# A recurrent-attention and spatial-gating kernel whose instructions are issued from a table: the table is replaced

## The chip, the cores and the metric

The kernel runs on one core of one Trainium2 chip. The core has five engines with a queue each: PE (TensorE, matmuls), DVE (VectorE), ACT (ScalarE), POOL (GpSimd) and SP (SyncE, which here issues every DMA). Each engine takes its instructions strictly in the order in which they were issued to it. PEld is PE's loading of the stationary operand. The metric is device time in microseconds (us), lower is better.

## What is computed

Batch 4, 8 heads, 768 steps, head size 48. The first half is a recurrence over time with a decaying state, the second a gated MLP that mixes over time:

```python
for t in range(S):
    cur = einsum('bhd,bhe->bhde', u * k[t], v[t])
    y[t] = einsum('bhd,bhde->bhe', r[t], state + cur)
    state = w[t][..., None] * state + einsum('bhd,bhe->bhde', k[t], v[t])
x = y.transpose(0, 2, 1, 3).reshape(B, S, H * D)          # 4 x 768 x 384
h = maximum(x @ w_in, 0)                                  # 384 -> 1024
u_, v_ = h[..., :512], h[..., 512:]
v_n = (v_ - mean(v_)) / sqrt(var(v_) + 1e-6)
v_s = einsum('ts,bsd->btd', w_spatial, v_n) + b_spatial[None, :, None]
out = (u_ * v_s) @ w_out                                  # 512 -> 384
```

## The kernel before

**Attention in slots.** Time is cut into 6 chunks of 128 steps per batch, 24 slots in all (i = 6b + c). A slot loads W, kk, rr and v from DRAM (`slot_load`; W, kk and rr have two buffers each), and from the seventh slot on also N, a natural copy of r and k. `slot_prep` makes a scan of W forwards and backwards on DVE (F, L414; pa, L422), multiplies kk and rr by them (L427, L429), and makes the diagonal term dg. For the first six slots dg comes from a product rk (L396) and a small matmul pg (L401); afterwards from N by two products and a sum (L435, L437, L438). dg is spread over a diagonal tile As by ACT or POOL (L458 or L453). `slot_a` is the matmul pa of kk and rr (L472), whose lower triangle DVE copies into As (L477). `slot_y` multiplies As by v into the accumulator pyw and, for all but a batch's first slot, adds the state's part (all L512). `slot_kt` transposes kk (pt, L492; copied to KT, L496), `slot_s` makes the state's increment pd (L550), adds and scales it (S, L556 to L562) and copies it to Sd (L566). `slot_x` splits y into an upper and a lower half xT (ACT, L579; for the first eight slots PE subtracts, L582, and ACT copies, L585; later DVE, L587).

**Precision by halves.** Each dense product is three matmuls (`mm3`, L592 to L594): upper by upper, upper by lower, lower by upper half. Weights arrive as 64-bit numbers and are turned into halves on the chip by four or so elementwise steps (L334 to L341): wv and wu are the two halves of w_in, three row blocks each, wo is w_out, ws (from wst, L309 and L311) the spatial matrix.

**The MLP.** `hv_unit` (one per slot) makes ph from xT and wv (L592 to L594, 512 columns), its ReLU hv and its row sums on ACT (L621 to L624); every third one normalizes three hv and splits them into vh and vl (L641 to L664). `g_unit` makes, for a half of a batch's time and a quarter of the 512 features, pu (from xT and wu; ReLU to us, L689) and pv (from vh, vl and ws, six steps), adds the bias (t, L698, on DVE, which frees pv's accumulator), multiplies by us (L700) and splits into gh and gl (L702, L703). `out_unit` makes po from gh, gl and wo, copies it (ot, L718) and stores it. ph, pu, pv, po, pt, pd and pg share four PSUM buffers.

**The check of w.** For 16 pairs of batch and head group the kernel loads w again (Nw, one buffer, shared with N and rk) and ACT takes the excess over 1 (L383). If the check fails, a general branch computes everything anew; with these inputs it is not taken.

**What sets the order.** All work is first recorded as 1805 steps, each with a list of engines that may run it. `PLAN` has one word per step: a letter for the engine (T is PE, V DVE, A ACT, G POOL, S SP) and a start in hundredths of a microsecond in base 36. Steps are sorted by these starts and issued in that order; the starts set the order and nothing else at run time, since each instruction still waits by semaphore for its inputs and its buffer. `fill` also reads them: up to the step `last` (after hv of the sixth slot), it puts matmuls on zeros (L791, called filler here, two passes each) into gaps that the table shows on PE.

```python
            o.on, o.start = w[0], int(w[1:], 36) / 100
            assert o.on in o.eng
        return sorted(self.ops, key=lambda o: o.start)
```

Of the kernel before, what the change touches and what calls it, by code (L numbers as in the profile page):

```python
# [33 lines left out]
V3gd V3lg A3n4 V3yy S3dz A3oj V40i V4ku V4pu A5yd V60d S216 A2xy V4tb V4ud V4w0 A4zf V50x S3ay V541 V56k
V5b2 V5g4 A5uz V5wk T20y T22w T25d A27z A2a9 A2ax Seh Sg9 Si1 S16t Gq3 Tuc Vlu Gpe Vrb Vu9 Vts Axt Gtm Vyv
Aym A1et Az9 Gzp T11e V157 V17o Tor V148 G1aj A1c4 A1h1 Tzt A13l T1rn T1sy T1u9 A20v T24v A266 T285 T2je
T2ld A2nz A2ri A2s5 Sjt Spm Svf S18c G12s T172 V10s G16c V177 V1a6 V19p A1gh G171 V1dp A1bb A1fn G1c3 A1t4
T1hc V276 V246 T1ee V266 G2b9 A2ec A2dd T1g4 A1i0 T2ae T2fv T2h6 A2lp T2o9 A2q6 T2s5 T2w3 T2zx A32j A34t
A35h A3x2 G392 V41h G44p G45d G460 G46o G47b V48b A4fr V4re A4ad A4cq G4f4 V4z4 A50u G57j S19u S1d4 S1wd
S1uf G27q T2bz V296 V2du V2ed V2ff V2ey A2n1 G2h2 V2iy A2gq A227 A2hd G2kl T2p1 V2uw V2sv T1ke V2kv G2nj  # L40
A2wz A2w0 T2nb V2r5 T2yc T35r T372 A3rk T3ty A463 T4ct T4fp T4i6 A4mh A4or A4pf S1p1 S1qt S2ja S2hc G2qu
T31v V2np G2ud V2ww V2xh V3ay A3h5 G2v2 V392 V3bf G2oy A3ct A3ij T3c1 V3p1 V3n0 T2ud V3bw G3r8 A3sw V3y8
T39a A3bc T47z T49a T4al A4ef T4ho A4it T4ul T4x2 T4z0 A52j A54t A55h S2l2 S2rz S396 S378 G3hx T3ug V3hx
G3qj V3re V3sf V3ry A3wi G3n0 V3vz A3za A3hp A3zy G4dc T3yh V45d V4fa T3f3 V4du V4j1 A4li V4k4 T4kp T4o0
T4pb A4rx T4wk A4y3 T50z T55u T57t A5as A5d2 A5dq A5g9 V5ho V5i3 V5im G5j6 G5jt G5kh G5l4 V5o9 A5qn V5sf
V5v2 A5wo V5yg A5ml A5oy V64q T5sr S3yw A47i S4aj A4tt S4y1 A57x S5ay A5jq T3gt T3r1 T3sh A3v6 T5ra T5t1
T5uh T5xe T61s T692 V6cz G6fv A6ls V72g T3ia T3l7 T3pk A3tv T5yv T60b T638 T64p T665 T67m V6bf G6d2 A6g1
V6io T3jq T3mn T3o4 A3q8 T5vy T6ja T6kq T6m7 T6nn T6p4 V6r8 G6vf A6z5 G773 T41j T430 T44g A4hg T6aj T6bz
T6dg T6ew T6gd T6ht V6po G6sn A6vl V73z T7qg T7rw T7td T7uu V7xm S7zc T76b T77r T7el T93h A95p S977 T87a
T88q T8g6 T8hn A8jr S8l9 T52x T54e T59r A5h2 T6tq T6v7 T6x5 T74u T7d5 T94y V988 G9eh A9qt V9sc T5b8 T5co  # L50
T5e5 A5ie T99b T9as T9c8 T9lq T9n6 T9om V9uc V9xo Aa02 Ga1p T5fl T5ii T5kx A5tn T9k9 T9q3 T9vg T9xv Tb0f
Tb1w Vb40 Vb5n Abbj Vbd1 T5h2 T5md T5nu A5sc T96e T97u T9is T9zb Ta0s Ta28 Va4c Vaby Aadl Gafe Tbix Tbke
Tblu Tbna Vbpf Sbrn Tarm Tat3 Tbg0 Tbhg Abjr Sbl8 Tc4b Tcdt Tcf9 Tcgq Ackl Scm2 S313 S3h0 S4f3 S5mr S4dk
V41x V47v V49t V4ae V4pd A4t9 G49t V4mg V66n V68a V69x A4ko A6bj A6hg T4rj V6fy V6nn T4er V4hb T6qu T6s5
A6u4 T6wn A6xt T71y T798 T7b6 A7ds A7g3 A7gq S3x4 S41x S4rf S6bl S4ph V57j G5nk V5pr V6k7 V5qc A6nr G5cl
V6w8 G6k7 V75j V776 G5lo A78s G79v T6yw V7du V7bt T4ma V4oe G5pr V5uc V5rc T5jz V5lk T7i2 T7jd T7ko A7n9
T7py A7r4 T7wa T7y8 T807 A82t A85k A868 S4gv S4uh S4w9 S78u S6tm V6ss G6y8 V6z3 V7g0 V6zn A7jk G6yx V7jk
G7hg G7ke V7pm G7d2 A7tc G7to T7mw V7z6 V7vm T5pk V61x G7bn V7ow A7ol T73w A75i T82g T83q T852 A89m V8ea
T8j4 T8l2 T8n0 A8pm A8se A8t1 A8wt V91u V9la G9lt V9o4 G9on V9pd V9px V9qg A9s8 G9u5 A9tx A9yd Val4 V9z8
Aa1h Ga4i S6nt S71u S7mx S7rm S7le V7lg G7pm V7r4 V81c V7u9 A850 V86s V84w G808 G835 V8cb A7si G8hc A8eo  # L60
T8be V8l4 V8j3 T7gc V7rl V7so A88o V8gm T8a6 A8bs T8p9 T8qk T8rv A8vh V8ww T902 T9rk T9ti A9w6 Aa61 Aa6p
S7jm S7pu S889 S8g4 S86q V88v G8cf V8dt V8na V8ft A8ru G8d4 V8qu G8oq G8ro V8yg A8du A901 G929 T8u3 V967
V947 T8eg V8hc G8j4 V914 V8w6 T9wx Va0q T9dy T9fa T9gk A9l5 V9ml Ta8r Tb3c Tb5a Ab9c Abcy Abf2 S84y S8ec
# [862 lines left out]
```

## Time and profile before

| | |
|---|---|
| median of 3 runs | 394.87 us |
| lowest, highest | 392.95, 396.45 us |
| span of the profiled execution | 390.9 us |
| instructions in it | 9006 |
| busy: PE, DVE, ACT, POOL | 370.4, 253.2, 198.6, 145.4 us |
| moved by DMA | 47.67 MB |

The span runs from the first to the last instruction of one execution that the hardware profiler recorded. The timed runs are separate executions, and their times also hold what lies around the span. In the profile, "busy" is the time in which at least one instruction of an engine ran; a matmul's end is modelled, and consecutive matmuls overlap, so PE's busy time also covers short waits. Rows of instructions read: start, length, engine, line, operation, output<-inputs, shape, count, and in brackets how long the engine stood idle before and what released it. Rows of groups read: line, engine, operation, names, shape, count | busy time, mean length in ns | idle time before them, with what ended it. In both, buffer numbers are left out of names.

### The profile page before, as it was taken

How to read it: one execution, taken by the hardware profiler on the slowest of the kernel's cores; microseconds unless marked ns; L12 is line 12 of the kernel's file. 1: busy time of each engine (PE TensorE's matmuls, PEld its weight loads, DVE VectorE, ACT ScalarE, POOL GpSimd, SP SyncE). 2: the span in 40 equal slices, each digit the busy share in tenths (PEclk: the TensorE clock that was granted, in tenths of full speed). 3: DMA queues.
4: the chain of work that ended last, by engine and by line, in shares of the span. 5: the costliest groups of instructions: out<-in, count | busy, mean ns of one | idle time of the engine just before them, and what ended most of it. 6: DMA issues, size and time to landing. Idle time of an engine off the chain costs nothing.

```text
span 390.9 us, 9006 instructions
## 1 busy us (share of the span) xinstructions
PE 370.4 (95%) x3546; PEld 336.2 (86%) x3546; DVE 253.2 (65%) x474; ACT 198.6 (51%) x526; POOL 145.4 (37%) x195
## 2 busy tenths in 40 slices
PE   7887998899999999999999998999999999999993
PEld 6776797689887888999989986889997899999993
DVE  5786789768879767289886477887564642324140
ACT  2465875886365484653356365357245533531121
POOL 3333756154744643255542227316412301414000
PEclk9869999999999999999999999999999999999998
DMA  7996465652255446345443464354133200010102
GB/s 202 277 299 180 112 194 150 184 164 71 72 170 175 129 112 205 110 132 160 127 114 122 130 177 136 114 162 122 58 108 115 76 15 9 0 60 3 62 2 70
DMA packets 33012, 47.67 MB, mean 122 GB/s; under 512 B 3264, under 2 KB 21824, under 8 KB 32960
## 3 DMA queue, kind: packets, MB, share of 16 engines
q1 hardware_dynamic: 32960, 47.00, 41.5%
q8 instruction: 30, 0.49, 0.5%
q14 instruction: 22, 0.18, 0.2%
HBM read 42.27 MB, written 4.72 MB: 120 GB/s over the span
## 4 chain that ended last, share of the span: by engine, by line
PE 68%; DMA 16%; ACT 4%; DVE 4%; issue 3%; POOL 2%; SPq 1%; ACTq 0%; DVEq 0%; POOLq 0%
PE pyw L512 7%; PE pv L592 7%; DMA Nw<-in_gt_dram 7%; PE pv L594 7%; PE pv L593 7%; DMA rr<-in_tr_dram 6%; PE pa L472 4%; PE po L592 4%; PE po L594 3%; PE po L593 3%; PE pu L592 3%; PE ph L592 3%; PE pu L593 3%; PE pu L594 3%; PE ph L594 3%
## 5 line engine op out<-in xcount | busy, mean ns | idle before, releaser
L592 PE MATMUL pv<-ws,vh 128*128 128x384 f32 x192 | 65.7, 342 | 0.0
L594 PE MATMUL pv<-ws,vl 128*128 128x384 f32 x192 | 64.4, 335 | 0.0
L593 PE MATMUL pv<-ws,vh 128*128 128x384 f32 x192 | 64.3, 335 | 0.0
L458 ACT ACTIVATE As<-ident,dg 128x128 f32<-128x128 f32 x112 | 35.5, 391 | 24.6 <-DVE dg L438 17.3
L477 DVE COPY_PREDICATED As<-mask,pa 128x512 f32<-128x512 int32 x48 | 33.9, 731 | 10.9 <-PE pa L472 7.1
L698 DVE TENSOR_TENSOR t<-pv,b_sb 128x384 f32<-128x384 f32 x32 | 17.6, 554 | 32.4 <-PE pv L594 31.7
L592 PEld LDWEIGHTS pv<-ws,vh 128*128 128x128 f32 x192 | 36.0, 188 | 1.4 <-issue 0.8
L593 PEld LDWEIGHTS pv<-ws,vh 128*128 128x128 f32 x192 | 36.1, 188 | 0.3
L594 PEld LDWEIGHTS pv<-ws,vl 128*128 128x128 f32 x192 | 36.0, 188 | 0.0
L592 PE MATMUL pu<-xT,wi 128*128 128x384 f32 x96 | 33.8, 353 | 2.1 <-DVE t L698 1.4
L592 PE MATMUL po<-wo,gh 128*128 128x384 f32 x96 | 33.0, 344 | 0.7 <-ACT KT L496 0.7
L414 DVE TENSOR_TENSOR_SCAN F<-zz,W 112x512 f32<-112x512 f32 x24 | 29.2, 1217 | 6.2 <-DMA W<-in_tr_dram 3.9
L594 PE MATMUL po<-wo,gl 128*128 128x384 f32 x96 | 32.3, 337 | 0.0
L594 PE MATMUL pu<-xT,wi 128*128 128x384 f32 x96 | 32.3, 336 | 0.0
L593 PE MATMUL po<-wo,gh 128*128 128x384 f32 x96 | 32.3, 336 | 0.0
L593 PE MATMUL pu<-xT,wi 128*128 128x384 f32 x96 | 32.2, 335 | 0.0
L702 ACT CAST gh<-t 128x384 fp32r<-128x384 f32 x32 | 16.3, 510 | 28.0 <-DVE t L700 16.7
L472 PE MATMUL pa<-rr,kk 48*128 48x128 f32 x384 | 28.5, 288 | 1.5 <-POOL ws L311 0.9
L592 PE MATMUL ph<-wi,xT 128*128 128x512 f32 x72 | 29.6, 411 | 0.2 <-DVE S L558 0.2
L422 DVE TENSOR_TENSOR_SCAN pa<-zz,W 112x512 f32<-112x512 f32 x24 | 29.4, 1226 | 0.4
L472 PEld LDWEIGHTS pa<-rr,kk 48*128 48x128 f32 x384 | 23.9, 191 | 5.8 <-issue 3.8
L594 PE MATMUL ph<-wi,xT 128*128 128x512 f32 x72 | 28.4, 394 | 0.0
(183 smaller groups left out, 838.8 us busy)
## 6 DMA issues: line engine op xcount, KB each, us to landing
N<-in_nat_dram SPq DMA_DIRECT2D x18, 384.0 KB, 3.2
Nw<-in_gt_dram SPq DMA_DIRECT2D x16, 384.0 KB, 3.5
W<-in_tr_dram SPq DMA_DIRECT2D x24, 224.0 KB, 3.2
kk<-in_tr_dram SPq DMA_DIRECT2D x24, 224.0 KB, 3.4
rr<-in_tr_dram SPq DMA_DIRECT2D x24, 224.0 KB, 3.7
v<-in_nat_dram SPq DMA_DIRECT2D x24, 192.0 KB, 3.1
out_dram<-ot SPq DMA_DIRECT2D x24, 192.0 KB, 2.1
wst<-in_w_spT_dram SPq DMA_DIRECT2D x12, 192.0 KB, 5.0
```

Of the source, the lines that this page charges most:

```text
L414: op({"V": 1.24}, lambda: nc.vector.tensor_tensor_scan(flat(F()[:R])[:, ::-1], flat(zz[:R])[:, ::-1], flat(W())[:, ::-1], 0.0, ALU.max, AL ...
L422: op({"V": 1.24}, lambda: nc.vector.tensor_tensor_scan(flat(E()[:R]), flat(zz[:R]), flat(W()), 0.0, ALU.max, ALU.mult), r=[(W, 0), ("zz", ...
L458: e.mul(As()[:, g, :], ident, dg()[:, 2 * g + j:2 * g + j + 1])
L472: nc.tensor.matmul(pa[j]()[:, g, :], kk()[rs, g, :], rr()[rs, g, :], start=True, stop=True)
L477: op({"V": 0.725}, lambda j=j, As=As: nc.vector.copy_predicated(As(), mask.unsqueeze(1).broadcast_to([P, G, C]), pa[j]()), r=[(pa[j], 0)], ...
L512: nc.tensor.matmul(py()[Q * n:Q * (n + 1), k_, :], a, b, start=n not in started, stop=not left[0], skip_group_check=True)
L592: nc.tensor.matmul(ps, ah, bh, start=first, stop=False)
L593: nc.tensor.matmul(ps, ah, bl, start=False, stop=False)
L594: nc.tensor.matmul(ps, al, bh, start=False, stop=last)
L698: op({"V": dve(HT)}, lambda: nc.vector.tensor_tensor(t1(), pv()[:, :HT], b_sb[:, tsl], ALU.add), r=[(pv, 0), ("b", 0)], w=[(t1, 0)])
L702: op({"A": act(HT)}, lambda: nc.scalar.copy(gh(), t1()), r=[(t1, 0)], w=[(gh, 0)])
```

## The change

Only `PLAN` changes; the number of steps, what they compute and their buffers are the same. Lines move up by four. One row of the table, before and after:

```diff
-T0 S4n S97 S1sk S1lz Sag Ak2 Vxp V1fm V1io A1nn V1yf Slk Av7 V1mi V1qr V1ul A1xg V20c S12r A1d3 V1pl V1so
+T11l S7s S6o S38f S3an Sb4 Avg Vxx Vzt V112 A14j V16f Sfk V19r V1b1 V1cw V1e5 A1fq G1hr Sgo A1h6 V1mc V1va
...
```

221 steps change engine. The net moves: DVE runs 22 more steps (487), POOL 12 fewer (168), ACT 10 fewer (365); PE keeps its 605 and SP its 180. Among them seven of 24 products kk by F go from POOL to DVE net (L427), six of 36 products on N (L435, L437), two of six rk (L396), and four of 24 copies ot from ACT to DVE. Diagonals As go from ACT to POOL net by four. Filler falls from 44 matmuls to 36. On PE, neighbouring steps of which one is dense (ph, pu, pv, po) and one is not fall from 105 to 83 pairs.

The first place is SP's queue at the start of the program, where loads are issued. Before:

```order
L319 DMA d_('wv', 0)_143<-in_w_in_dram 128x1024
L366 DMA W1_149<-in_tr_dram 112x4x128
L369 DMA kk1_171<-in_tr_dram 112x512
L369 DMA rr1_173<-in_tr_dram 112x512
L366 DMA W2_182<-in_tr_dram 112x4x128
L319 DMA d_('wv', 1)_188<-in_w_in_dram 128x1024
L369 DMA kk2_222<-in_tr_dram 112x512
L319 DMA d_('wu', 2)_227<-in_w_in_dram 128x1024
L369 DMA rr2_247<-in_tr_dram 112x512
L308 DMA wst5_0_249<-in_w_spT_dram 128x384
L319 DMA d_('wu', 0)_263<-in_w_in_dram 128x1024
L319 DMA d_('wv', 2)_289<-in_w_in_dram 128x1024
```

And now, after W0, rr0 and kk0:

```order
L365 DMA kk1_136<-in_tr_dram 112x512
L822 DMA up_sb_106<-in_gu_dram 48x4x1 x2
L365 DMA rr1_140<-in_tr_dram 112x512
L362 DMA W1_142<-in_tr_dram 112x4x128
L315 DMA d_('wv', 0)_144<-in_w_in_dram 128x1024
L369 DMA v0_148<-in_nat_dram 128x384
L315 DMA d_('wu', 2)_150<-in_w_in_dram 128x1024
L369 DMA v1_152<-in_nat_dram 128x384
L315 DMA d_('wv', 1)_155<-in_w_in_dram 128x1024
L315 DMA d_('wv', 2)_162<-in_w_in_dram 128x1024
L362 DMA W2_164<-in_tr_dram 112x4x128
L365 DMA kk2_221<-in_tr_dram 112x512
```

All three blocks of wv are now ahead of the third slot's W2, kk2 and rr2; before, wv2 came behind them.

The second place is PE's queue where the third slot's pg2 stands. Before, between y of slot 0 and pd of slot 1:

```order
L512 MATMUL pyw_83<-As0_1_190,v0_138 32x128 x4
L512 MATMUL pyw_83<-As0_1_190,vp0_113 32x128 x4
L791 MATMUL pyw_83<-zk_78 128x128
L401 MATMUL pg2_313<-up_sb_106,rk2_291 128x2 x4
L791 MATMUL pyw_83<-zk_78 128x128 x5
L550 MATMUL pd1_347<-v1_309,KT1_293 64x48
```

And now:

```order
L588 MATMUL ph0_0_368<-wi0_117,xT0_0_0_295 128x512
L589 MATMUL ph0_0_368<-wi1_118,xT0_0_0_295 128x512
L590 MATMUL ph0_0_368<-wi0_117,xT0_0_1_349 128x512
L508 MATMUL pyw_83<-As1_1_299,v1_152 32x128 x4
L508 MATMUL pyw_83<-As1_1_299,vp1_114 32x128 x4
L508 MATMUL pyw_83<-rr1_140,Sd_111 32x128 x12
L397 MATMUL pg2_403<-up_sb_106,rk2_388 128x2 x4
L488 MATMUL pt2_418<-ident_85,kk2_221 128x112 x4
```

pg2 now stands behind the first two ph steps of the first slot and all of slot 1's y; before, it stood ahead of pd1, of pa2, of y of slot 1 and of every ph. Ahead of the rows shown now stand 14 fillers in one piece (28 passes), between y of slot 0 and pa1.

The third place is ACT's queue at the ninth check of w, Nw8, some 215 us into the trace of before. Before:

```order
L383 ACTIVATE Nw8_2806,over_123<-Nw8_2806,neg_94 128x768
L702 CAST gh1_1_0_2857<-t11_1_0_2839 128x384
L383 ACTIVATE Nw9_2845,over_123<-Nw9_2845,neg_94 128x768
L621 ACTIVATE hv2_3_2897,st2_1_2898<-ph2_3_2787 128x512
L623 ACTIVATE st2_1_2898<-st2_1_2898 128x1
L383 ACTIVATE Nw10_2884,over_123<-Nw10_2884,neg_94 128x768
```

And now:

```order
L379 ACTIVATE Nw8_2804,over_123<-Nw8_2804,neg_94 128x768
L714 COPY ot1_0_1_2877<-po1_0_1_2773 128x384
L714 COPY ot1_0_2_2888<-po1_0_2_2758 128x384
L454 ACTIVATE As17_0_2895<-ident_85,dg17_2798 128x128 x4
L441 COPY vp1_114<-v17_2756 128x4x2x16
L698 CAST gh1_1_0_2912<-t11_1_0_2836 128x384
L637 ACTIVATE st2_0_2610<-st2_0_2610,eps_92 128x3
L422 COPY zz_80<-zk_78 112x4
L379 ACTIVATE Nw9_2900,over_123<-Nw9_2900,neg_94 128x768
```

More of ACT's other work now stands between one check and the next.

More of the change, by code (lines that the diff above doesn't have):

```diff
@@ L34 @@
[L34 to L63, printed above, removed]
@@ new lines @@
+A2yf G3oo S2n4 V4lx V4n6 V4tu V4vp A54j G5cd S2hk A3kp V3mj V4ur V4wn A57y V59k S4fi V4qb V4rk V4xk V50b A529
+V5mi T1ix T1lk T27l A2af A2cp A2e4 Sa0 S5k S8w Seg Gnq Trl Vo5 Vzl V10r V120 V164 A1ai Gtq V183 Vxp A1ap Ayc
+A170 T1a9 V1f3 V1hd Tw0 Vyv G128 A13u V1gw Txn A1b9 T1he T1nh T1p0 A1rj T1uh A1w7 T1xt T21e T2mi A2p9 A2t2
+A2tp Sjw Sry St2 S12b V1o8 T1qw V1j6 V1o0 V1rk V1s4 V1z1 A213 V1pw V21k A219 A25e G224 A21w T23q V27e V297
+T1e1 V1n9 G1rs A1td A1u2 T1tl A1x9 T29s T2bi T2cr A2g8 T2hu A2mr T2of T2qc T2s9 A2wi A30p A31c A37j G3aw V390
@@ new lines @@
+G39r G3bo V3cf V3cx V3dh A3pn A3s0 V3v6 A3lu A3o7 G3x3 V3g0 A3tg V4o4 S15n S1e0 S1rl S1ux G277 T2en V237 G2ao
+V2bf V2bz V2f5 A2ha G2ds V2fh A2im G2o3 G2jh A2j9 T2ib V2nv V2y3 T1zq V2h4 V2pn A2r6 A2vt T2lc A2rv T2zp T318
+T32i A3f2 T3ij A3jn T3or T3qo T42t A45n A47x A48k S1w1 S27g S2fc S2io V2t9 T2vm V2hx V2t1 V313 V329 V35f A37e
+G2yb V37d A30z G3a7 A382 A3bk T3j0 V3of V3q8 T2y2 V30c V3f0 V3ng V3ny T34d A366 T3sl T3u4 T3vd A3ya T422 A43g
+T452 T4es T4h6 A4jy A4m9 A4mw S2js S367 S353 S337 V3iy T3m1 V398 V3d5 V3fr V3s1 V3km A3vl V3kv V3wv A3vs G43w
@@ new lines @@
+G40k G428 T3z1 V42p V459 T3x9 V44i G45s V47u V47d T46z T48i T49r A4ca T4gp A4ht T4jz T4lw T4nt A4qd A4so A4tb
+A4vs V505 V519 G520 V52r V53a G540 G54s A5gk A5ix V5kt V5av A5kd V5ph V55j A5ct V5i4 T97y S3pg A40u S43y A4f6
+S4ia A4wb S4zf A5a8 T2u6 T3e7 T3fn A3hq T5nj T5oy T5qe T5ru T5ta T5w7 V5ya G62o A65m G72r T35j T4bn T4dc A4iv
+T5hq T5km T5m2 T5ur T5xn T5z3 V69o G6fa A6ky V6ou T36z T39v T3bb A3g4 T60j T61z T63f T64v T66b T67r V6kl G6qe
+A6td G77r T38f T3cr T3h3 A3w2 T5eu T5ga T5j6 T6fr T6h7 T6in V6lw V6nj A6qa G6t2 T7m9 T7nq T7p6 T87f A89i S8hc
@@ new lines @@
+T79b T7aq T7dm T7f2 V7ro S7ue T77u T7c6 T85z T88v V8sx S9g2 T4pq T4r6 T4sm A516 T6nx T6pd T6qt T6s9 T6tp T6v6
+V74c V8kk A8ma G8o0 T4zx T52t T549 A56v T8if T8jv T8lb T926 T93m T9cy V9jc V9kz A9mp V9tt T51d T58l T5a1 A6ui
+T952 T96i T9u9 T9vp T9yl Ta01 Va7k Va97 Aamm Vao7 T55p T575 T5d4 A5fh T8ab T8br T8d7 T8fj T8gz T8mr V92y G94t
+Aa8o Gaar Tawi Tb0a Tb1q Tbdb Vbxa Sdnl Tbrx Tbtn Tbzf Tc0v Ac2y Sc4j Taht Taqq Tas6 Tav2 Vax5 Sb38 S37b S3mr
+S3xy S5dc S3zm V3yj G49v V4am V4bf V4b6 A4f0 G4cz V4ew V5o6 V5r6 V5tt A5lt G5wp G5yc T4u2 V623 V60a T4j3 A4p0
@@ new lines @@
+T697 T6aq A6cn T6f1 A6ge T6k3 T6m0 T6wm A6z6 A71g A723 S3vo S452 S4ki S5vl S4b8 V4gk V4k2 V5zl V64b V69g A6a3
+V4k9 V67s G66j G6cl V6fk G6bw A6hg A6m3 T6c0 V6q6 V6rz T4x4 V4ze G5gp A5ni A6pl T4yr A55o T6zf T70y T727 A74q
+T774 A79a T7gj T7if T7kd A7mw A7vl A7wz S5eg S50j S5i2 S6hc S6cp V6b0 G6hy V6io V6tr V6wx A6xk V6ix V71d G6x1
+G702 V731 G772 G75f A75s T743 V7bj V79q T5bh V5jt G6vq A7b1 A7ac T6yj V75n T7qm T7s5 T7te A7vx V7xf T7zy T825
+T842 A86m A8ak A8b7 A8do V8sr V8rg G8s7 V8xq G8yi G8za G902 A988 A9iv G9vd A94g A9ef G9h5 V9f5 Aa0b Gbp7 S67y
@@ new lines @@
+S6ig S74s S770 S75w V6y8 G7f7 V7fy V7gr V7gi A7kc V7db V7k8 G7kd G7ne V7qe A7fy A7s3 G7sw T7va V8f7 V8d6 T7yb
+V80l G89b V8be V8aw T8en A8g6 T8pv T8re T8sn A8vj V8xy T994 T9b1 T9ee A9gy A9kh A9wj S784 S7ta S7vz S7s6 S80o
+V7mq G7uk V7va V8he V8ey A8kz V87f V8p1 G834 V864 V8bv G90i G8dp A8s1 T8uj V94i V9bv T8o7 V8qp G8t6 V9gf A97j
+T988 V9do T9hy T9jh T9kr A9nu V9pd Ta4d Ta6a Ta87 Aaar Aad2 Aadp S7ke S8g8 S8v8 S8dn S8wc V8lw V8uk V90k V96q
+V94a A9kb V91a V9a7 V8us V8wf V8z9 G9mj A90y A9sc T9mm V9v5 Va5a T9gb V9il G9n8 A9vu Va73 Taa4 Tabn Tacx Aaft
@@ new lines @@
+Vahc Tajj Tamw Taot Aard Aatn Aaub Aaws Gax0 Vb6b Gb72 Vb8b Gb92 Gb9u Vbal Vbb4 Abms Gbvo Abhk Abpa Vbz8 Vbce
+Abf1 Gbh2 S911 A9bu S9ey A9pr S9sv Aa63 Sa97 Aak1 T8xk T8za T90q A96g Tbv3 Tbwj Tbxz Tcgs Tcj4 Tckk Vdf7 Vdtw
+Ady7 Gdzx T9pn Ta1h Ta2x Aa50 Tc2b Tc3r Tc57 Tc6n Tc9j Tcaz Vcd2 Vcep Acgg Vci1 T9rd T9st T9x5 A9z8 Tc83 Tccf
+Tcdv Tcfb Td2u Td4a Vdaq Vdsk Adx2 Veav Talg Tatm Taxy Ab01 Tcvc Tcx2 Tcyi Tczy Td1e Td5q Vd96 Gdb0 Advx Ve5v
+Tegg Tejd Tep4 Teth Aevk Sezr Teks Teqk Tes0 Tf4b Af6s Sf8d Tehw Tem8 Teno Tf2m Af7u Sfpj Tb37 Tb63 Tb7j Abgh
@@ new lines @@
+Tdxa Tdyq Te06 Te1m Te32 Te4i Veyu Vf0i Afcy Gfeo Tb4n Tber Tbg7 Abjj Tfz4 Tg0k Tg20 Tg3g Tg4w Tg6c Vg8f Vga2
+Agbt Vgmm Tb8z Tbaf Tbbv Abdy Tf8v Tfak Tfdg Tfex Tfgd Tfj9 Vflc Gfqv Afxc Ggwp Tfus Tg7s Tgdw Agi6 Tf5r Tfc0
+Tfht Tfoj Tfpz Tfrf Vfto Ggju Agor Vgru Tht2 Thui Thvy Thxe Ahzh Skkj Tguo Tgwe Th60 Th7g Vha2 Shtx Tgzr Th17
+Th8w Thac Ahii Sij8 S8l2 S9h6 S9nc San5 S9rh V9qo G9yu V9zk Va05 Va3a Aa9t G9za Va3m Gay3 Vb12 Vb2p Ab7x Gb4j
+Ab4f Taes Vb6j Vbdo Taze Vb40 Tbkg Tblz Abo8 Vc62 Tdev Tdnp Tdtg Ae01 Ae3v Ae4i S9ad S9qd Safi Sb4h Sagm Vaai
@@ new lines @@
+Gafw Vagm Vbfg Vbly Abmm Vae0 Vbiy Vbkn Gbmi Vbph Abqq Gbso Ac4o Tbn9 Vbuo Vcg1 Tbhn Vbqs Vcb9 Vcol Acky Tbja
+Vbm7 Tcp1 Tcqk Tcrt Acuc Vcwq Tdh2 Tdiz Tdls Adoc Adt6 Adtt Sb24 Sb10 Sbk7 Sbr9 Sbny Vbri Gbv7 Vbwh Vc0x Vbx1
+Ac4i Gc4w Vc4f Gc27 Vcjd Vcl0 Gcqz Gcmu Gcs8 Tcm0 Vd1n Vcu6 Tbqa Vcqq Vcvy Vcy1 Acx5 Tci7 Acjq Td76 Td8p Td9z
+Adch Vdgi Tdpm Tdrj Tdvd Ae1y Ae48 Ae6m Afe3 Ge9b Vfi7 Gfiy Gfjq Vfmn Gfnd Gfo5 Afow Ag1t Vghd Vfow Ag3y Vhej
+Ag5e Agm8 Ggo9 Sbj3 Sbsd Scue Scms Scvi Vc84 Vcrs Vd3g Vd40 Vdah Adb4 Vcp3 Vd7i Vcyi Gd1w Vdht Addj Gdjn Gdla
@@ new lines @@
+Tdbu Vdlt Vdnm Tctp Vczt Vd0w Vdwv Adzc Tdkw Admf Tean Tec6 Tedf Aefy Veon Tfkp Tfmm Tfsv Afvf Agrg Ags4 Scwm
+Scpq Sdck Sdjl Sddo Vdc1 Gdfq Vdj4 Vdpf Vdll Adsz Vdxc Vdv7 Ve4k Ve77 Ve8u Aeh0 Aeaj Gecx Te7m Veei Vemu Te5y
+Vea4 Gera Veyd Vexw Tefb Veh3 Texy Tezh Tf0q Afqv Vfse Tgpq Tgxu Th2n Ah8o Ahay Ahwg Sd7n Sdmh Seg0 Seam Seh4
+Vdzf Veil Vej4 Vejp Vesw Aetk Ve2w Vepy Gelk Geol Verl Afce Af8w Gf21 Teux Vfcu Vf3z Tf77 Vfif Gfk6 Ag39 Vfq5
+Tg98 Tgar Tgc1 Agej Vgg2 Thn2 Thp8 Thr5 Ahtp Ahvz Ai0j Ai31 Vi34 Vi7e Vikj Vil3 Gilu Gine Viog Vitk Aiv9 Gixa
@@ L115 @@
+Ar3h Vr52 Tprt Tq0h Tq1x Aq40 Tq9g Tqaw Tqds Tqi4 Tqjk Tqnw Vqpz Vqrm Aqtc Vqvw Tr59 Tr6p Tr85 Tr9l Vrbo Srdh
+Tqzh Tr2d Trdx Trfd Arhg Srj1 Tr0x Tr3t Trb1 Trch Arek Srg5 Vnk1 Tq4u Vqx8
 """
```

84 lines of the change are left out of this document (29 added, 55 removed).

## The prediction, made before the changed kernel was run

> **What bounds the kernel now.** I read the page first, then the stages, then the chain that ended last, then the waits and loads that the chain names. The sum is made against the profiled execution: its span is 390.9 us, and the median of the three timed runs, 394.87 us, stands 4.0 us above it; I carry these 4.0 us over.
>
> ```profile
> span 390.9 us, 9006 instructions
> ...
> 0.00:36.44 36.44, 29.11 (x298) 26.19 (x299) 23.98 (x47) 18.11 (x46) 11.90 (x27) 0.86 0.91 246
> 36.44:130.00 93.56, 89.71 (x988) 77.14 (x987) 79.12 (x135) 61.36 (x170) 50.99 (x65) 1.00 0.49 142
> 130.00:220.00 90.00, 90.00 (x877) 82.67 (x876) 61.89 (x126) 47.33 (x129) 39.15 (x53) 1.00 0.47 137
> 220.00:300.00 80.00, 77.03 (x745) 69.20 (x742) 57.11 (x104) 40.90 (x107) 28.35 (x30) 1.00 0.42 124
> 300.00:384.60 84.60, 84.55 (x650) 81.02 (x648) 31.12 (x66) 30.39 (x74) 15.04 (x21) 1.00 0.09 31
> ```
>
> After each stage's length stand the busy times of PE, PEld, DVE, ACT, POOL, then granted clock and DMA share. PE is the bound: from 130 to 220 and from 300 on it has no hole. It has 3.85 us of holes in 36 to 130, 2.97 in 220 to 300, and the first 36 us are a stage of another kind: the clock is 0.86, and DMA is at 0.91. So the question is how much PE time is not needed matmul. The chain gives what one step of each kind takes (start, length, what):
>
> ```profile
> 36.68 0.23 PE ph L593
> 37.83 0.17 PE pyw L582
> 39.97 0.98 PE pg L401 x8
> 129.12 1.09 PE pa L472 x16
> 130.21 0.37 PE pu L592
> ...
> 151.62 1.67 PE pyw L512 x56
> 166.41 0.39 PE pt L492 x4
> 168.90 0.60 PE pd L550 x14
> 172.68 1.01 PE pyw L512 x32
> 384.37 0.19 PE po L594
> ```
>
> A dense step is three matmuls: 0.52 us for pu, pv and po (0.17 each; 384 steps, 199.7 us), 0.70 for ph (three of 0.23; 72 steps, 50.4). Attention per slot: pa 24 x 1.09 = 26.2; y with the state 20 x 1.67 = 33.4, without it 4 x 1.01 = 4.0; pd 20 x 0.60 = 12.0; pt 20 x 0.39 = 7.8; pg 6 x 0.98 = 5.9; eight L582 steps about 1.4. Sum 340.8. The last matmul ends at 384.37 + 0.19 = 384.56, so 43.8 us of PE are not needed work. The end behind it (copy, store, closing) is 390.9 - 384.56 = 6.3 us and stays: both tables end on po steps that ACT copies out.
>
> Where the 43.8 us lie: the first ph starts at 36.44.
>
> ```profile
> 11.78 7.07 DMA rr<-in_tr_dram
> ...
> 18.99 1.28 POOL rk L396
> ...
> 20.31 1.87 PE pg L401 x8
> 22.18 2.34 PE pyw L791 x10
> ...
> 29.07 0.47 ACT xT L585
> ...
> 29.57 1.60 PE pyw L791 x12
> ...
> 31.88 1.28 ACT As L458 x4
> ...
> 34.61 1.83 PE pyw L791 x14
> 36.44 0.24 PE ph L592
> ```
>
> The third slot's rr lands at 18.85, its rk is made on POOL, and pg2 stands in PE's queue in front of everything else; later PE waits for ACT's xT, and ACT's queue waits for As. The L791 rows are filler on zeros. Needed work ahead of 36.44: pg, pt, pa and pd three times (3 x 3.06 = 9.2), one L582, y of slot 0 (1.0) and slot 1 (1.67): 12.0. Lost: 24.4 us, over half of the 43.8. The other 19.4 are the 6.8 us of holes above and what the busy times hide: the first matmul after an attention step is charged 0.37 instead of 0.17, and PE goes from attention to dense or back 105 times.
>
> **The change part by part.** No step is added or removed, but filler goes from 44 to 36 matmuls, and 221 steps change engine. Four things count.
>
> *Loads at the start.* Landings before, seen in who waited for them, and the sizes (KB after the count):
>
> ```profile
> W<-in_tr_dram SPq DMA_DIRECT2D x24, 224.0 KB, 3.2
> v<-in_nat_dram SPq DMA_DIRECT2D x24, 192.0 KB, 3.1
> d_('wv', 0)_143<-in_w_in_dram SPq DMA_DIRECT2D x1, 512.0 KB, 5.8
> ...
> 4.23 1.22 DVE L414 TENSOR_TENSOR_SCAN F<-zz,W 112x512 f32<-112x512 f32 x1 [2.42 <-DMA W<-in_tr_dram]
> 12.31 1.27 POOL L396 TENSOR_TENSOR rk<-kk,rr 112x512 f32<-112x512 f32 x1 [0.31 <-DMA rr<-in_tr_dram]
> 15.14 0.68 ACT L334 ACTIVATE e_('wv', 1)_245<-d_('wv', 1)_188 128x512 f32<-128x512 f32 x1 [3.37 <-DMA d_('wv', 1)_188<-in_w_in_dram]
> 23.52 0.70 ACT L334 ACTIVATE e_('wv', 2)_337<-d_('wv', 2)_289 128x512 f32<-128x512 f32 x1 [0.84 <-DMA d_('wv', 2)_289<-in_w_in_dram]
> ```
>
> Counting the KB issued up to each (W, kk, rr 224, v and wst 192, each wv and wu half 512): 224 to W0 by 4.2, 2048 to rr1 by 12.3, 2784 to wv1 by 15.1, 4960 to wv2 by 23.5; the last three are 178, 194 and 218 KB per us after the first issue at 0.8. In the new queue wv1 ends 3264 KB and wv2 3776, so they land at about 17 and 19; W1 (1344) at 8.4, or 9.4 if one more transfer is ahead of it; v0 (2048) at 12.3. rr2 comes at 4448 KB, 21 to 22, some 3 us later. Its rk2 is now made on DVE, and behind it in DVE's queue stand the last conversions of wv2, which every third ph step needs; pg2 itself no longer stands ahead of the ph steps.
>
> *The first ph.*
>
> ```profile
> L477 DVE COPY_PREDICATED As<-mask,pa 128x512 f32<-128x512 int32 x48 | 33.9, 731 | 10.9 <-PE pa L472 7.1
> ```
>
> From W1 at 9.4 DVE's queue is a scan (1.22), KT and two As (0.73 each, KT counted like an As): to 12.8. y of slot 0 runs to 13.9. Then come 14 fillers (28 passes: at 1.83/14 = 0.13 each 3.7 us, at 2.34/10 = 0.23 each 6.5), pa1 and L582: 19 to 21.7. ACT's lower half of xT, 0.47, follows; with pd1 and half of y1 PE reaches ph at 19.5 to 22.5; I take the middle, 21. Work ahead of it is then two each of pg, pt, pa, pd (6.1), 1.0, 0.5 and L582: 7.8. Lost: 13.2 instead of 24.4, a gain of 11.2. The loads of slots 2 and 3 that were pushed back can take some back: none if the ph steps ahead cover pg2 and pa2, the whole 3 us that rr2 is later if not. I take 1.5, the middle. Net 9.7; bounds 0 (PE waits for the loads all the same) and 12.7 (ph at 19.5, nothing given back).
>
> The clock is the open end of this step. [...]
>
> *Holes from 36 on.* In the later stage the chain runs through the check of w (Nw), which ACT reads from one buffer:
>
> ```profile
> 216.61 3.60 DMA Nw<-in_gt_dram
> ...
> 221.35 3.02 DMA Nw<-in_gt_dram
> ...
>   DMA Nw<-in_gt_dram: 19.1, 13
> ...
> 238.16 0.44 PE L592 MATMUL pu<-xT,wi 128*128 128x384 f32 x1 [1.35 <-DVE t L698]
> ```
>
> ACT stood 19.1 us in 13 waits with us, gh and xT queued behind the Nw step; what they hold up reaches PE as the 1.35 us hole. A round of the one buffer is load and ACT step, 4.74 us from 216.61 to 221.35; before, one ACT step stands between Nw8 and Nw9 and two between Nw9 and Nw10, now seven and four. I count 3 of the 2.97 us here as gone (a little more than the holes show hides in the matmul ends, a little stays), and 3 of the 3.85 in 36 to 130, where rr and kk loads now stand earlier relative to use. Bounds for the two: 0 and 7.
>
> *Switches.* PE goes between attention and dense 83 times instead of 105; 11 fewer returns at 0.37 - 0.17 = 0.2 each save 2.2; bounds 1 and 2.2; I take 2.
>
> *Engines.* The largest move is kk times F from POOL to DVE, seven times:
>
> ```profile
> L427 POOL TENSOR_TENSOR kk<-kk,F 112x508 f32<-112x508 f32 x19 | 21.0, 1108 | 11.6 <-DVE rk L396 4.2 <-PE ph L594 3.3 <-DVE pa L422 1.5
> L427 DVE TENSOR_TENSOR kk<-kk,F 112x508 f32<-112x508 f32 x5 | 4.1, 825 | 0.0
> ```
>
> That shortens the way to pa by 0.28 us each (1108 to 825 ns). In all 22 more steps stand on DVE (487 for 465), at 0.83 each at most 18 us more than the 253 that its stages sum to. PE's dense steps cover this: I book 0. If that cover is gone, an eviction of pv queued behind such a step costs PE up to 0.83.
>
> Sum: 9.7 + 3 + 3 + 2 = 17.7; span 373.2, time 394.87 - 17.7 = 377.
>
> **The rivals.** *The start is bound by the loads, whatever the order.* For it: DMA share 0.91 there. Against: PE was held by its queue, with wv data on chip by 24. If nothing is gained at the start, 377 + 9.7 = 387. *Nothing new waits and the rest of the holes goes too*: first ph at 19.5 and no 1.5 given back (3 us), and 4 us of what the busy times hide: 370. *The holes only move*: start and stages both refill, because PE's order is as tight as before and other waits end last: 395. *DVE becomes the bound, slower.* Place: the 32 pv evictions (L698), which free the accumulators that PE fills next. If a moved product stands ahead of each and PE waits for it, 32 x 0.83 = 26.6 against 17.7 gained: 404. It decides from 0.68 us per eviction (17.7 + 4 over 32); for it stand 79.12 us of DVE in the 93.56 of the second stage, against it one single 1.35 us hole in the whole trace of before. [...]
>
> **How the numbers follow.** My sum (372 to 383): 0.52. All holes gone (365 to 372): 0.18. Start bound by loads (383 to 390): 0.11. Holes only move: 0.10. DVE bound: 0.09. The measurement tells about 1% from no change, 4 us, so faster (under 391) is 0.52 + 0.18 + 0.11 = 0.81, same 0.10, slower 0.09. The range 365 to 390 leaves out the last two.
>
> **What would show it.** First ph near 21 us and no more than two pg steps before it: the start step is right; at 30 or later it is wrong. [...] Nw waits of ACT well under 19.1 and no hole of over 1 us in 220 to 300 show the third step. DVE waits of PE (pu, pv, po or ph released by t L698) summing to over 10 us would make the whole wrong, and so would PE holes in 36 to 130 above 4.

## The result and the profile after

| | median | lowest to highest | runs |
|---|---|---|---|
| before | 393.91 us | 390.94 to 396.45 | 4 |
| after | 376.57 us | 376.26 to 377.17 | 4 |

The ratio after to before is 0.957, with an interval of 0.952 to 0.962. The prediction was 377 us in a range of 365 to 390. The profiled execution spans 374.5 us, 16.4 less than the one of before. The ratio, here and below, leaves out executions that took over 1.5% longer than the fastest of the same kernel, and the medians are over all.

The stages of the trace after, cut as in the prediction (length, then busy time of PE, PEld, DVE, ACT, POOL, granted clock, DMA share):

```profile
0.00:36.44 36.44, 31.61 (x378) 26.85 (x380) 31.43 (x61) 20.16 (x56) 16.55 (x32) 1.00 0.78 228
36.44:130.00 93.56, 90.94 (x959) 81.35 (x956) 80.38 (x154) 62.62 (x168) 38.83 (x58) 1.00 0.55 163
130.00:220.00 90.00, 90.00 (x947) 82.63 (x946) 69.16 (x128) 44.80 (x123) 33.40 (x47) 1.00 0.51 145
220.00:300.00 80.00, 80.00 (x869) 73.20 (x868) 54.66 (x103) 43.19 (x119) 29.82 (x37) 1.00 0.37 107
```

The holes of 220 to 300 are gone, those of 36 to 130 went from 3.85 to 2.62 us, and the clock of the first stage is 1.00 where it was 0.86. DVE works 31.43 of the first 36.44 us where it worked 23.98, about as much as PE with its filler (31.61). The clock column starts at the first clock record (6.85 us in after, 6.37 in before) and shows 1.00 ahead of it, though a filler pass takes 0.21 us there and 0.11 behind it.

The start on PE, from the timeline (start, length, instruction, in brackets the idle time before it and what ended it):

```profile
11.11 0.64 PE L546 MATMUL pd<-v,KT 128*64 128x48 f32 x16 [0.20 <-DVE KT L492]
...
15.88 3.17 PE L787 MATMUL pyw<-zk 128*128 128x128 f32 x26 [1.54 <-ACT xT L575]
18.97 1.16 PE L468 MATMUL pa<-rr,kk 48*128 48x128 f32 x16
...
22.29 0.50 PE L588 MATMUL ph<-wi,xT 128*128 128x512 f32 x1
```

The first ph starts at 22.29 us, with two pg steps before it. The filler ran at 3.17/26 = 0.12 us a pass, at a granted clock of 1.00, but 26 of its 28 passes waited 1.54 us for ACT: filler is written into the tile pyw, where y stands too, and ACT's step that reads y there (the upper half of xT, 15.35 to 15.82) stood in ACT's queue behind other work.

To see where the time went I use one count in all that follows: for an amount of needed work (the durations of the prediction's first part, 340 us in all), the time at which PE has issued it, less that work. This is what PE has lost by then.

| needed work issued | 35 us | 100 us | 180 us | 260 us | 335 us |
|---|---|---|---|---|---|
| lost before | 27.6 | 34.8 | 37.1 | 43.6 | 44.6 |
| lost after | 20.6 | 23.2 | 25.4 | 27.4 | 28.4 |
| lead gained in the stretch | 7.0 | 4.6 | 0.1 | 4.5 | 0 |

With the prediction's own durations, 340.8 us in all, the leads at these marks are 8.0, 11.6, 11.8, 16.3 and 16.3 us instead of 7.0, 11.6, 11.7, 16.2 and 16.2: the curve of after steps up by 1 us right at 35 us of work, so the first stretch is worth 7 to 8 us and the second about 4.

Three stretches carry the 16.2 us: the start, the stage that follows it, and the one in which ACT waited for Nw.

### The profile page after: what moved, and what is told of

The parts are those of the page before. It is cut to its first block, busy times and chain, and to the rows that moved or that the text cites. A ratio compares the mean times of both kernels' runs of the same rounds, so it can differ in the third digit from the quotient of the medians.

```text
span 374.5 us, 8921 instructions
## 1 busy us (share of the span) xinstructions
PE 360.8 (96%) x3530; PEld 330.9 (88%) x3530; DVE 259.2 (69%) x496; ACT 189.7 (51%) x504; POOL 127.8 (34%) x183
## 4 chain that ended last, share of the span: by engine, by line
PE 86%; DVE 7%; ACT 1%; issue 1%; DMA 1%; POOL 1%; SPq 0%; DVEq 0%; POOLq 0%
PE pv L588 9%; PE pv L590 9%; PE pv L589 9%; PE pyw L508 8%; PE pa L468 6%; PE po L588 5%; PE po L590 4%; PE po L589 4%; PE pu L588 4%; PE ph L588 4%; PE pu L590 4%; PE pu L589 4%; PE ph L590 4%; PE ph L589 4%; PE pd L546 3%; PE pt L488 2%
## 5 line engine op out<-in xcount | busy, mean ns | idle before, releaser
L589 PE MATMUL pv<-ws,vh 128*128 128x384 f32 x192 | 64.3, 335 | 0.0
L454 ACT ACTIVATE As<-ident,dg 128x128 f32<-128x128 f32 x96 | 30.5, 391 | 17.0 <-PE pyw L508 8.8
L698 ACT CAST gh<-t 128x384 fp32r<-128x384 f32 x32 | 15.9, 511 | 44.1 <-DVE t L696 25.6
L589 PEld LDWEIGHTS pv<-ws,vh 128*128 128x128 f32 x192 | 36.1, 188 | 0.4
L696 POOL TENSOR_TENSOR t<-t,us 128x384 f32<-128x384 f32 x15 | 15.8, 1057 | 49.0 <-DVE t L694 27.9
L589 PE MATMUL po<-wo,gh 128*128 128x384 f32 x96 | 32.3, 336 | 0.0
L589 PE MATMUL pu<-xT,wi 128*128 128x384 f32 x96 | 32.2, 336 | 0.0
L449 POOL TENSOR_SCALAR_AFFINE_SELECT As<-dg 128x512 f32<-128x512 f32 x24 | 17.1, 722 | 35.2 <-DVE dg L434 18.9
```

The lines of the kernel that those rows point to most:

```text
L449: e.affine_select(out=As(), in_=dg()[:, j::2].unsqueeze(2).broadcast_to([P, G, C]), pattern=[[0, G], [1, C]], compare_op=ALU.is_equal, fil ...
L454: e.mul(As()[:, g, :], ident, dg()[:, 2 * g + j:2 * g + j + 1])
L589: nc.tensor.matmul(ps, ah, bl, start=False, stop=False)
L698: op({"A": act(HT)}, lambda: nc.scalar.copy(gh(), t1()), r=[(t1, 0)], w=[(gh, 0)])
```

## The experiments

Each kernel was timed beside the kernel before on the same chip; the ratio is to that (after itself: 0.957). Gains below are worked out from the ratios and 394.5 us, the median of before there, so they may differ a little from the difference of two medians.

| kernel | median us | ratio, interval |
|---|---|---|
| new_to_35 | 389.84 | 0.988, 0.982 to 0.994 |
| new_to_70 | 382.85 | 0.967, 0.960 to 0.973 |
| new_to_131 | 379.23 | 0.960, 0.955 to 0.966 |
| old_to_74 | 388.72 | 0.981, 0.975 to 0.987 |
| new_order_old_engines | 395.04 | 1.003, 0.998 to 1.007 |
| old_order_new_engines | 408.08 | 1.040, 1.033 to 1.048 |
| old_engines_act | 380.58 | 0.966, 0.958 to 0.974 |
| old_engines_pool_dve | 386.61 | 0.982, 0.973 to 0.992 |
| more_on_dve | 380.42 | 0.969, 0.965 to 0.973 |
| old_two_N | 391.84 | 0.992, 0.988 to 0.997 |
| new_two_N | 378.12 | 0.960, 0.952 to 0.968 |
| no_fill | 379.00 | 0.963, 0.956 to 0.970 |

### Which part of the table earns what

Four kernels hold both tables and go from one to the other at a time CUT, at places where nearly the same steps lie behind both orders; OLD is the table that takes over, and LAG shifts its starts. For the first three the table of after comes first (LAG is 3.93 and 5.15 in the second and third):

```diff
+CUT, LAG = 35.01, 1.3
...
-        for o, w in zip(self.ops, words):
+        for o, w, u in zip(self.ops, words, OLD.split()):
             o.on, o.start = w[0], int(w[1:], 36) / 100
+            late = int(u[1:], 36) / 100
+            if o.start >= CUT:
+                o.on, o.start = u[0], max(CUT + late / 1e4, late - LAG)
```

> The new table up to its 35.01 us, by when 21 us of needed matmul are issued, then the remaining steps in the old order on the old engines. At equal needed work the new trace is 7.1 us ahead of the old one there (its whole lead is 16.6 at the end). Theory (each part of the table earns its own share, and the lead of the start is kept): last matmul 7 us earlier than before (about 377.5), time about 387. Rival (the lead of the start is lost again, since the old order after it waits for loads and conversions that the new start put off): last matmul within 2 us of 384.6, time 392 to 395.

> The new table up to its 70.14 us (56 us of needed matmul), where the two orders have almost the same set of steps behind them, then the old order and the old engines. The lead at this work is 9.7 us. Theory (shares add up, the lead is kept): last matmul about 375, time about 384, so that more than half of the whole gain comes from the first fifth of the work. Rival (the gain is one of the whole, and a start without its rest is refilled): 390 or more.

> The new table up to its 131.17 us (116 us of needed matmul), then the old order and engines. Lead at this work 11.6 us. Theory (shares add up): last matmul about 373, time about 382; the 5 us that are left of the lead, 3 of them at 220 to 240 us of the old trace where ACT waits for Nw, stay with the old order. Rival (the later holes were a consequence of the old start and go by themselves): 377 to 378.

The fourth is the converse (table of before first, CUT 74.07, LAG -3.93).

> The converse: the old table up to its 74.07 us, then the new order and the new engines. Theory (shares add up): the old start keeps its loss, the rest earns 16.6 - 9.7 = 6.9 us: last matmul about 377.7, time about 387. Rival (holes only move: the new rest fits only the new start): 391 or more.

Against 394.5 the ratios are gains of 4.8, 13.1 and 15.7 us for the three, 17.0 for the whole table, and 7.5 for the converse. 13.1 + 7.5 = 20.6 is near the whole 17.0 within the intervals, so around 70 us the parts add up, and the rivals that the lead is refilled fall for the cuts at 70, 74 and 131 us. Two expectations were off. The table up to 131 earned 15.7 and not 11.6, with 380.9 as the upper end of its interval where 382 was expected; the profiled execution of before, from which my 11.6 was read, was quicker than the median one (below), and the four runs of new_to_131 had high mean clocks (0.990 to 0.999). By its time alone that run lies as near to its rival (377 to 378) as to the theory.

The cut at 35 us earned 4.8 where 7 was expected, and its trace shows that here the rival holds in part. At 21 us of needed work new_to_35 leads before by over 7 us, at 30 us of work by 1. Behind the cut ACT's queue comes to a conversion of wst and waits 5.02 us for its load; Sd stands behind it, and PE waits 2.01 us for Sd:

```profile
43.09 0.51 ACT L399 CAST ws<-wst 128x384 fp32r<-128x384 f32 x1 [5.02 <-DMA wst<-in_w_spT_dram]
...
46.46 0.86 PE L602 MATMUL pyw<-rr,Sd 112*32 112x128 f32 x24 [2.01 <-ACT Sd L656]
```

The clock from 40 to 60 us is 0.83, where it is 1.00 in after. So the 4.8 is the start's gain less what this cut costs, and the difference to 13.1 doesn't tell how much the new order earns between 35 and 70 us.

The stage 220 to 300 shows what is left to the late part, in new_to_131 and then in old_to_74:

```profile
220.00:300.00 80.00, 78.50 (x789) 70.67 (x791) 55.23 (x115) 41.99 (x113) 28.76 (x32) 1.00 0.39 114
```

```profile
220.00:300.00 80.00, 79.89 (x819) 72.96 (x818) 55.10 (x105) 44.34 (x122) 32.58 (x40) 1.00 0.46 131
```

With the old order in this stage a hole of 1.5 us stays; with the new one 0.11. That speaks for the theory: part of the late loss stays with the old order.

### Order or engines

The prediction booked the 221 changed engines at 0. In two kernels one order goes with the other's engines:

```diff
-        for o, w in zip(self.ops, words):
-            o.on, o.start = w[0], int(w[1:], 36) / 100
+        for o, w, u in zip(self.ops, words, OLD.split()):
+            o.on, o.start = u[0], int(w[1:], 36) / 100
```

> The new order with each step on the engine that it had before (221 steps go back). Theory (the gain is one of order, the engine moves are worth 0): 376 to 379. Rival (the moves carry part of the gain, since the order was laid out for them; kk times F back on POOL costs 0.28 us each on the way to pa, and a POOL step holds a DVE step behind it): 382 or more, with new PE holes at 20 to 60 us.

> The old order with the new engines. Theory (moves worth 0): 392 to 396. Rival (the moves alone bring a part of the gain): 390 or less; or, since the old order was laid out for the old engines, slower than 398.

The theory fell in both. By the ratios the new order alone gains nothing (395.04 us), the new engines alone cost 16 us (408.08), and together they gain 17. Two more kernels put back one half of the moves each, by the test `"A" in o.eng` (the step may run on ACT) and its opposite:

```diff
-            o.on, o.start = w[0], int(w[1:], 36) / 100
+            o.on, o.start = (u if "A" in o.eng else w)[0], int(w[1:], 36) / 100
```

> The new order; each step that can run on ACT (100 of the 221 moved ones: building and copying As, KT, Sd, vp, dg, norm and ot) stands on its old engine, the 121 moved between POOL and DVE stay on their new ones. With all 221 put back the time was 395. Theory A (POOL to DVE carries the gain: in that run POOL made prod, rk, kk times F and S one after the other from 23.40 to 27.69 us, and ACT's Sd and xT and PE's ph waited behind it): 378 to 382. Theory B (the ACT moves carry it): 388 to 395. Theory C (each set fits only with the other, as the old order with the new engines at 408 suggests): 386 or more here, and as much in the converse.

> The converse: new order, the 121 steps moved between POOL and DVE on their old engines, the 100 that can run on ACT on their new ones. Theory A (POOL to DVE carries the gain): 388 to 395. Theory B (the ACT moves carry it): 378 to 382. Theory C (only together): 386 or more.

Over after's 376.57, the 100 steps put back on or off ACT cost 4.0 us and the 121 between POOL and DVE 10.0; both together 18.5. That is 4.5 us more than the sum, which the intervals of the ratios (about 1% each way for the two halves) don't tell from none. So mostly theory A: the first lies in its band, the second 1.4 us below it, and theory C, which asked for 386 or more in both, falls with the first. Of the 4.0 us a part is the clock: the two runs of old_engines_act at a mean clock of 0.991 and 0.995 took 379.22 and 378.99, some 2.5 us over after. Of what old_engines_pool_dve lost by the end over after (39.0 to 28.4), 8.4 us were lost by 35 us of work.

What happens there is to be seen in new_order_old_engines. Its first ph comes at 22.20, as early as in after (22.29), and yet it has lost 28.9 us by 35 us of work, against 20.6. In its file L503 is prod, L481 rk, L512 kk times F, L647 S, L651 Sd, L670 the lower half of xT and L876 filler. POOL's queue, then two rows of ACT's and one of PE's:

```profile
23.40 0.31 POOL L503 TENSOR_SCALAR prod<-F 112x4 f32<-112x4 f32 x1 [9.24 <-DVE F L499]
23.68 1.28 POOL L481 TENSOR_TENSOR rk<-kk,rr 112x512 f32<-112x512 f32 x1
25.03 1.75 POOL L512 TENSOR_TENSOR kk<-kk,F 112x508 f32<-112x508 f32 x1
26.74 0.95 POOL L647 TENSOR_TENSOR S<-S,prod 112x192 f32<-112x192 f32 x1
```

```profile
27.72 0.72 ACT L651 COPY Sd<-S 48x192 f32<-48x192 f32 x2 [2.07 <-POOL S L647]
...
29.03 0.47 ACT L670 CAST xT<-pyw 128x384 fp32r<-128x384 f32 x1
```

```profile
29.55 2.08 PE L876 MATMUL pyw<-zk 128*128 128x128 f32 x8 [1.93 <-ACT xT L670]
```

The same steps in after stand on DVE (first fence), then POOL and ACT:

```profile
23.57 0.16 DVE L414 TENSOR_SCALAR prod<-F 112x4 f32<-112x4 f32 x1
23.64 0.68 DVE L392 TENSOR_TENSOR rk<-kk,rr 112x512 f32<-112x512 f32 x1
24.36 0.87 DVE L423 TENSOR_TENSOR kk<-kk,F 112x508 f32<-112x508 f32 x1
```

```profile
23.88 0.81 POOL L558 TENSOR_TENSOR S<-S,prod 112x192 f32<-112x192 f32 x1 [0.97 <-DVE prod L414]
```

```profile
25.64 0.72 ACT L562 COPY Sd<-S 48x192 f32<-48x192 f32 x2
...
26.96 0.47 ACT L581 CAST xT<-pyw 128x384 fp32r<-128x384 f32 x1
```

The short step S stands in POOL's queue behind rk and kk times F of the next slot, and comes at 26.74 instead of 23.88. ACT's Sd waits for S, xT stands behind Sd in ACT's queue, and PE's ph needs xT: 2 us later at xT, 3 at ph (31.28 against 28.39). The same chain, with S at 27.48 and the same wait of PE, stands in old_engines_pool_dve, and not in old_engines_act, whose longest wait for xT L670 is 0.7 us; so it belongs to the 121 moves between POOL and DVE:

```profile
27.48 0.95 POOL L647 TENSOR_TENSOR S<-S,prod 112x192 f32<-112x192 f32 x1
...
30.29 2.07 PE L876 MATMUL pyw<-zk 128*128 128x128 f32 x8 [1.93 <-ACT xT L670]
```

In both kernels PE comes out of this wait at half pace, so that the wait is in effect paid twice: the 8 filler passes behind it take 2.08 and 2.07 us, 0.26 each where after's took 0.12, and in new_order_old_engines the clock falls to half at 28.9 us, within the wait. A wait as long as this one, 1.99 us up to 15.79 in new_order_old_engines, left the clock at 1.00, so the wait alone doesn't settle it. One stretch of the stages, in new_order_old_engines and then in after:

```profile
29.50:36.60 7.10, 7.05 (x46) 5.40 (x46) 3.82 (x7) 4.44 (x13) 5.50 (x5) 0.56 0.45 127
```

```profile
29.50:36.60 7.10, 7.10 (x115) 5.56 (x112) 6.88 (x11) 6.43 (x22) 6.92 (x8) 1.00 0.66 183
```

PE is busy in both, but at 0.56 a matmul of ph takes 0.63 us (L678 at 31.85) where after takes 0.40 (L589 at 28.71). These rows show the chain for the moves as a set; prod, rk and kk times F of this one slot were not put back by themselves, so what they alone are worth stays open. And of the 18.5 us that putting all moves back costs, some 10 are lost behind 35 us of work, where no chain was followed.

### Whether DVE is close to being the bound

```diff
+            if o.on == "G" and o.eng["G"] in (1.02, pool(508)):
+                o.on = "V"
```

> The new table with 30 more full steps moved from POOL to DVE: the 12 products kk times F and the 18 products on N that POOL still has, some 25 us more of DVE (259 to 284). Theory (dense steps cover DVE, engine moves are worth 0): 376 to 379. Rival (DVE is nearly the bound, as its 36 of 40 us in 40 to 80 says): each early step shows on PE, 3 to 8 us, 380 to 385; all of them on the path would be 400.

It cost 3.9 us over after, 0.13 for each of the 30 steps. That is above the theory's band and at the small end of the rival's: a full step more on DVE mostly hides, and does not cost the 0.6 to 0.7 us that it takes (592 to 734 ns, by group, in this trace). The lost time by 35 us of work is 23.1 (after 20.6), by the end 32.4 (28.4): over half of it at the start again. In this trace the clock of the first 36.44 us was also 0.95, and the filler from 17.77 on took 0.21 us a pass, against 1.00 and 0.12 in after, and the first ph came at 24.23, so 0.13 us a step is rather too much.

### The buffer of Nw

```diff
-        w = buf(p2, [P, 2, DM], "N", f"Nw{n}", 1)
+        w = buf(p2, [P, 2, DM], "N", f"Nw{n}", 2)
```

and the same for N and rk, which share the tag; in old_two_N with the old table, in new_two_N with the new one.

> The old table with two buffers in place of one for the tag that Nw, N and rk share, so that the load of the next Nw need not wait for ACT's step on the last. Theory (the one buffer's round of load and ACT step makes the PE hole at 220 to 240 us): ACT's wait for the Nw load falls from 19.1 us to under 8, the matmul lead at the end is 3 us, time about 391.5. Rival (the hole is made by the order of ACT's queue, whatever the load does): PE busy in 220 to 300 stays at 77 of 80 us and the time at 394.

> The new table with two buffers for the tag of Nw, N and rk, as tried with the old one, where two buffers took the time from 394.55 to 391.84. Theory (the new order has already spread the Nw steps, so the two changes earn the same 3 us once): within 1 us of 376.6, PE without a hole in 220 to 300 as before. Rival (they add up, since ACT still waits 6.5 us for Nw loads in the new trace): 374 or less, below both kernels.

In old_two_N, ACT's row of waits and the stage 220 to 300 (of an execution with a mean clock of 0.970):

```profile
ACT Nw L383 <- DMA Nw<-in_gt_dram: 8.8, 7, 2.2
```

```profile
220.00:300.00 80.00, 79.37 (x768) 72.05 (x767) 57.24 (x105) 41.11 (x106) 29.56 (x31) 1.00 0.44 128
```

The wait fell from 19.1 to 8.8 us (under 8 was expected), the hole from 2.97 to 0.63, and the time by 0.8% or 3.0 us (1.1 to 4.9). So the round of the one buffer, of the tag that Nw shares with N and rk, did make the hole. In new_two_N the wait fell further, to 3.7, and nothing was gained, though the median of 378.12 lies 0.5 us above the theory's band: its two runs at a clock of 0.992 and 0.995 took 376.71 and 376.99, its two at 0.983 and 0.985 took 379.50 and 379.25. So the rival of 374 falls, and the order and the second buffer earn these 3 us once. No kernel tried was below the changed one.

### Filler and the clock

```diff
-GAP, FILL_TO = 0.3, 5
+GAP, FILL_TO = 9e9, 5
```

> The new table without the filler matmuls on zeros (34 of the 36 go; the one at the head of the program and the one that ends the fill stay). Theory (filler holds the granted clock up): the clock of the first 36.44 us falls from 1.00 to below 0.85, the first ph from 22.36 to 24 or later, time 380 to 386, as the run with the same start whose clock was 0.79 in the first 20 us stood at 384. Rival (DVE's queue sets the start, and the 26 passes from 15.88 to 19.05 only hold pa1, whose rr was ready at 17.5): first ph at 22.4 or earlier, time 374 to 377.

Neither band held the 379.0. The first stage and the first ph in no_fill, and the first pg there and in after:

```profile
0.00:36.44 36.44, 26.54 (x291) 20.88 (x295) 29.65 (x57) 18.49 (x50) 14.14 (x30) 0.91 0.76 223
```

```profile
24.06 0.80 PE L588 MATMUL ph<-wi,xT 128*128 128x512 f32 x1
```

```profile
7.28 1.86 PE L397 MATMUL pg<-up_sb,rk 112*128 112x2 f32 x8 [7.28 <-POOL rk L392]
```

```profile
7.45 0.95 PE L397 MATMUL pg<-up_sb,rk 112*128 112x2 f32 x8
```

The 0.91 is too high a figure: the first clock record of this trace is at 16.80 us, and up to there PE ran at half pace, as the pg step shows, which took 1.86 us where it takes 0.95 in after. If the 9.5 us from 7.28 to 16.80 count as half, the mean is 0.78. So clock (below 0.85) and first ph (24 or later) came out as the theory had them, and only the time lies 1 us below its band. The lost time at the end is 30.7, 2.3 more than after, so all the filler together is worth some 2 us. Whether the long block in the middle helps is open. In after rr of slot 1 was ready at 17.51 and pa1 stood behind the filler until 18.97; without filler pa1 came at 19.64, but there the steps ahead had run at half pace and rr itself was ready only at 19.53.

## Why the prediction was right, and where not

**The total.** 377 against 376.57. Two small errors cancel: the span was forecast at 373.2 and is 374.5, and of the 4.0 us carried over between span and median only 1.8 are fixed (time less span is 1.7 to 1.9 in every run whose span is listed, after's 376.26 and 374.5 among them). The other 2.2 are then what the profiled execution of before was quicker than the median one. It had a mean clock of 0.984; 32 runs of before lie between 0.957 and 0.993, with a median of 0.974.

**The start, booked at 9.7 net.** The mechanism is right in its main part: rr2's pg no longer stands in PE's queue, and the first ph came at 22.29 (taken 21, range 19.5 to 22.5). That is read from the traces; no kernel moved pg2 or the loads alone. Lost ahead of the first ph are 14.5 us (22.29 less 7.8) instead of 24.2 (36.20 in the timeline, less 12.0), so 9.7 gross for 11.2 booked. The middle of the range hid two errors. The filler ran at the fast pass (0.12 us), and on the prediction's own path that puts the first ph at 19.5; it came 2.8 us later. 1.5 us of this is the filler's wait for ACT's xT, for which the sum had no term, and 1.4 us that pd1, two more fillers and half of y1 ran after L582 on PE (20.43 to 22.29) and not beside ACT's 0.47 us. By 35 us of work 7 to 8 are left: about 2 given back, for 1.5 booked, but not for the reason booked: between 22 and 36 us no engine's wait in after ends on a load. The signs named for this step were poor ones: new_order_old_engines shows both (first ph at 22.20, two pg before it) and gains nothing.

**Engines, booked at 0: the step that failed.** The prediction priced a moved step by its time on DVE and by the 0.28 us that kk times F becomes shorter. It did not ask what stands behind the step on the engine that it leaves. On POOL that was S, and through S, Sd and xT the next ph. Put back, the moves take all of the gain with them, so the 17.7 us that the text gave to order belong to order and engines together. That the total came out right all the same is because the moves of the table fit its order, which the prediction had not examined: in that it was lucky. The other half of that step holds: more DVE work is covered, at most about 0.13 us a step, and the rival of a DVE bound at 404 had little behind it. PE has no wait for the pv evictions in the new trace.

**Holes, 3 + 3.** In 220 to 300 the cause is shown (old_two_N). The holes went as booked, but the size was too small: the lead grows by 4.5 us between 180 and 260 us of work, of which the second buffer alone brings about 3. ACT's wait in the new trace:

```profile
ACT Nw L379 <- DMA Nw<-in_gt_dram: 6.5, 5, 2.4
```

In 36 to 130 the holes shrank by 1.2 us, not 3, while the lead grew by about 4 between 35 and 100 us of work. The rest is in matmul starts that came closer, not in holes; what brought them closer was not separated.

**Switches, 2.** Not separated by any run. PE changes between attention, dense and filler 33 times between 35 and 100 us of work before and 20 after, 22 and 23 times between 100 and 180; the lead grows by 4.6 in the first and by 0.1 in the second stretch. That agrees with a price on the change, but the first stretch has other causes too. Start, holes and switches together measured 7.0 + 4.6 + 0.1 + 4.5 = 16.2 for 17.7 booked.

**The clock, the open end of the start.** Right as an open end, too small as a size: its two filler passes, 0.13 and 0.23 us, put only 2.8 us between the earliest and the latest first ph of its sum. The order of new_to_70 is that of after up to 70 us of the table, but the filler block in its profiled execution took 5.26 us for 3.17:

```profile
7.66 1.02 PE L491 MATMUL pg<-up_sb,rk 112*128 112x2 f32 x8 [1.04 <-DMA up_sb<-in_gu_dram]
...
11.95 1.09 PE L640 MATMUL pd<-v,KT 128*64 128x48 f32 x16 [0.75 <-DVE KT L586]
...
17.41 5.26 PE L881 MATMUL pyw<-zk 128*128 128x128 f32 x26 [0.63 <-ACT xT L669]
22.60 1.16 PE L562 MATMUL pa<-rr,kk 48*128 48x128 f32 x16
```

Its first ph came at 25.92, 3.6 us later than after's. This is not new_to_70's alone. after and new_to_131 kept the full clock through the start, with the first ph at 22.29 and 22.12; new_to_70, new_two_N, more_on_dve and old_engines_act stood at half clock for 3.4 to 10.2 us before 22 us, with the first ph at 24.2 to 25.9. So differences of up to 4 us between these kernels are not clear of the clock. A straight line through the 25 runs of before that enter the ratios, which lie loosely about it, gives 1.4 us for 0.01 of mean clock; from 0.974 to after's 0.997 that is, as an estimate, about 3 of the 17 us. Part of the gain is thus a clock that stayed up in all four runs of after (0.993 to 0.997). How much of that belongs to the new order is open: new_two_N, with the same order, ran at 0.983 to 0.995, still above before's median. That no run of after fell to new_two_N's lower end, where 2.5 us more are lost, was luck.

**The rivals.** A start bound by the loads whatever the order (387) and holes that only move (395) did not come; 395 is the time that the order gives without its engines.
